# First batch of an attention-and-GLU kernel: q times kᵀv with 128 tokens a matmul, other warm matmuls, and a changed order of the first steps

## The chip, the cores and the metric

The kernel runs on one core of one Trainium2 chip, in fp32 throughout. The core has TensorE (matmuls, with a separate instruction that loads the stationary operand, the weights), VectorE, ScalarE, GpSimd and SyncE, which each take their instructions in order from a queue of their own, and 16 DMA engines. In the profile they are PE (matmul) and PEld (weight load), DVE, ACT, POOL and SP; a q behind a name is the engine's queue, where it issues a DMA or waits. The metric is the device time of one execution in microseconds (us). Of the kernel before, three executions gave 999.26, 999.58 and 1000.35 us, median 999.58.

## The reference

```
kv  = einsum('bhsd,bhse->bhde', k, v)            # 8 batches, 8 heads, 576 tokens, 64 wide
out = einsum('bhsd,bhde->bhse', q, kv)
rms = sqrt(mean(out * out, axis=-1) + 1e-6)
x   = out / rms * g_norm                         # to 4608 tokens by 512
y   = (sigmoid(x @ w_gate) * (x @ w_val)) @ w_out   # 512 -> 1536 -> 512
```

q, k and v come as float32. The three weights come as float64 and are passed as 64-bit words; the kernel makes float32 of them itself.

## The kernel before

The tokens are worked in chunks of 512 (`G`), nine of them. For all but the first chunk the two layers use a scheme with fewer products (`first_layer_fast`, L983, and `second_layer_fast`, L1085); the first chunk goes through plain matmuls of 128 by 512 (class `Plain`, L621, and `second`, L859), because the weights are still being converted then. The change touches only what comes before that: the attention of the first batch and the first conversions.

**Attention of the first batch.** Its eight heads are four pairs, n = 0 to 3, and `attention(n, ...)` has eleven steps for a pair. `KV` (L302) sums kᵀv over six groups of 96 tokens, one head on each half of the array's columns, and `KVO` (L306, VectorE) copies the result into `kvq`. `Q` (L312) transposes q through TensorE, and `QO` (L317, ScalarE) copies it to `qT`, with channels on partitions and tokens along the row. `U` (L329) multiplies: its stationary operand is a slice of `qT`, its moving operand the 64 by 64 kᵀv of one head, so the result has tokens on partitions. `SQ` (ScalarE), `SUM` (VectorE), `ROOT` (ScalarE) and `NORM` (VectorE, L346 and L348) make the norm; `X` (L356) transposes the result through TensorE, and `XO` (L365, ScalarE) copies it into `xT`, from which the layers read: pair m gives the m-th 128 channels. In `U` each matmul takes 64 tokens (`PH`): ten slices of tokens (`2 * NU`, the last one overlapping) for two heads, 20 matmuls of 64 by 64, in turn on the four quarters of the array.

**Warm matmuls.** `warmN` (L677) stands for N matmuls whose result nobody reads, with the 128 by 128 identity as both operands. They keep TensorE busy between real steps.

**Conversion.** Unit u is a staged pair of weight blocks (gate and value block of the same 128 hidden features, 128 by 512 each). Its five VectorE steps c.0 to c.4 (L195, L213, L225, L229, L236) and two ScalarE steps a.0 and a.1 (L200, L218) make float32 of it. `gu.i` and `vu.i` are the gate half and the value half of step i alone. Three staging buffers are in use; `w1` to `w4` (`load_unit`) issue the loads of units 1 to 4 on SP's queue, and `w3` and `w4` reuse the buffers of units 0 and 1. Later units are converted from `convert_step`, at places written out by hand among the plain matmuls.

**Order.** The string `order` (L654) fixes the order in which all this is recorded, and with that the order within each engine's queue. `b0.i.m` is one plain matmul of the first hidden block (i = 0 gate, 1 value; m the 128 channels it sums over, so it needs `XO` of pair m). After the string, the loop at L848 runs the plain matmuls of the other hidden blocks; block 1 needs unit 1 converted.

Of the kernel before, what the change touches and what calls it, by code (L numbers as in the profile page):

```python
# [10 lines left out]
FP32 = mybir.dt.float32  # L11
# [9 lines left out]
def kernel(  # L21
# [155 lines left out]
    def convert(u):  # L177
        kind, f = units[u]
        vec = nc.vector
        d = {}  # L180

        def s0(some=slice(None)):

            if kind == "gv":
                g, r = divmod(f, NF2)
                m = w1[:, r // 2, 2 * NMT * (r % 2):2 * NMT * (r % 2 + 1), g]
                for i, name in enumerate(("wg", "wv")):
                    w[name, f] = m[:, NMT * i:NMT * i + NMT]
            else:
                t = w2[:, f:f + 2, :]  # L190
                for i in range(2):
                    w["wo", f + i] = t[:, i]
                m = by_block(t.rearrange("p i f -> p (i f)"))
            d["m"] = m
            vec.tensor_scalar(out=m.bitcast(U32)[:, some], in0=words(u)[1][:, some], scalar1=0x000FFFFF, scalar2=None,  # L195
                              op0=ALU.bitwise_and)

        def a0():
            m = d["m"]
            nc.scalar.activation(out=m, in_=m.bitcast(U32), func=AF.Identity, scale=2.0 ** -20, bias=one)  # L200

        def s1(some=slice(None)):


            if "p" in d:
                t = None
            elif u < 15:
                t = raw.tile([P, UW], U32, tag="cz", name="cz", bufs=2)
            else:
                t = at_ps()[:, 0:2].rearrange("p r c -> p (r c)").bitcast(U32)  # L210
            if t is not None:
                d["p"] = by_block(t)
            vec.tensor_scalar(out=d["p"][:, some], in0=words(u)[1][:, some], scalar1=20, scalar2=0x7FF, op0=ALU.logical_shift_right,  # L213
                              op1=ALU.bitwise_and)

        def a1():
            p = d["p"]
            nc.scalar.activation(out=p.bitcast(I32), in_=p, func=AF.Relu, scale=2.0 ** 23, bias=exp_off)  # L218

        def s2():  # L220

            m = d["m"]
            if u > 2:
                load_unit(u - 1 + NST, (1,))
            vec.scalar_tensor_tensor(out=m, in0=words(u)[0], scalar=2.0 ** -52, in1=m, op0=ALU.mult, op1=ALU.add)  # L225

        def s3():
            p = d["p"]
            vec.scalar_tensor_tensor(out=p, in0=words(u)[1], scalar=0x80000000, in1=p, op0=ALU.bitwise_and,  # L229
                                     op1=ALU.bitwise_or)  # L230

        def s4():

            m, p = d["m"], d["p"].bitcast(FP32)
            if kind == "gv":
                vec.scalar_tensor_tensor(out=m, in0=m, scalar=g_col, in1=p, op0=ALU.mult, op1=ALU.mult)  # L236
            else:
                vec.tensor_tensor(out=m, in0=m, in1=p, op=ALU.mult)
            if u > 1:
                load_unit(u + NST, (0,))  # L240

        return {"c": [s0, s1, s2, s3, s4], "a": [a0, a1]}
# [48 lines left out]
    def attention(n, at_ps):  # L291

        b, m = divmod(n, NHP)
        d = {}
        kv = kvq[:, m // 2, m % 2]

        def kv_mm():
            d["kv"] = ps = at_ps("kv")
            for j in range(NJ):
                js = slice(HD * j, HD * j + HD)  # L300
                for e in range(2):
                    nc.tensor.matmul(ps[HD * e:HD * e + HD, 0, 0:HD], pairs[n]["k"][:, e, js], pairs[n]["v"][:, e, js],  # L302
                                     start=(j == 0), stop=(j == NJ - 1))

        def kv_out():
            nc.vector.tensor_copy(out=kv, in_=d["kv"][:, 0, 0:HD])  # L306

        def q_mm():
            d["q"] = ps = at_ps("q")
            for j in range(NJ):  # L310
                c0 = NP * (j % JH)
                nc.tensor.transpose(ps[:, j // JH, c0:c0 + NP], pairs[n]["q"][:, j].rearrange("p e d -> p (e d)"),  # L312
                                    ident[0:NP, 0:NP])

        def q_out():
            d["qT"] = qTs[:, S * (n % 2):S * (n % 2) + S]
            nc.scalar.copy(out=d["qT"].rearrange("p (i n) -> p i n", i=2), in_=d["q"][:, :, 0:JH * NP])  # L317

        def u_mm():


            ps = at_ps("u")
            d["u"] = ps[:, :, 0:NU * HD]
            for i in range(2 * NU):
                t0 = min(PH * i, S - PH)
                r = PH * (i % 2)
                for e in range(2):
                    es = slice(HD * e, HD * e + HD)
                    nc.tensor.matmul(d["u"][r:r + PH, e, HD * (i // 2):HD * (i // 2) + HD],  # L329
                                     d["qT"][es, t0:t0 + PH], kv[es], start=True, stop=True)  # L330

        def u_square():
            d["sq"] = sqs[:, NU * P * (n % 2):NU * P * (n % 2 + 1)].rearrange("p (e c) -> p e c", e=2)
            nc.scalar.activation(out=d["sq"], in_=d["u"], func=AF.Square)

        def u_sum():
            d["ms"] = sb.tile([P, 2, NU], FP32, tag="ms", name="ms")
            nc.vector.tensor_reduce(out=d["ms"].rearrange("p e i -> p (e i)"),
                                    in_=d["sq"].rearrange("p e (i d) -> p (e i) d", d=HD), axis=AX.X, op=ALU.add)

        def u_root():
            nc.scalar.activation(out=d["ms"], in_=d["ms"], func=AF.Sqrt, bias=eps, scale=1.0 / HD)

        def u_norm():

            nc.vector.reciprocal(d["ms"], d["ms"])  # L346
            d["xn"] = d["sq"].rearrange("p e c -> p (e c)")
            nc.vector.tensor_tensor(out=d["xn"].rearrange("p (i e d) -> p e i d", e=2, d=HD),  # L348
                                    in0=d["u"].rearrange("p e (i d) -> p e i d", d=HD),
                                    in1=d["ms"].unsqueeze(3).to_broadcast([P, 2, NU, HD]), op=ALU.mult)  # L350

        def x_mm():
            d["x"] = ps = at_ps("x")
            for i in range(NU):
                bank, c0 = divmod(P * i, UX)
                nc.tensor.transpose(ps[:, bank, c0:c0 + P], d["xn"][:, P * i:P * i + P], ident)  # L356

        def x_out():

            s0 = 0  # L360
            while s0 < S:
                c, o = divmod(S * b + s0, G)
                i, r = divmod(s0, UX)
                n_ = min(G - o, (UX if i == 0 else S - UX) - r)
                nc.scalar.copy(out=chunk(c)[:, m, o:o + n_], in_=d["x"][:, i, r:r + n_])  # L365
                s0 += n_

        return [kv_mm, kv_out, q_mm, q_out, u_mm, u_square, u_sum, u_root, u_norm, x_mm, x_out]
# [264 lines left out]
    def plain(c, u, ps, steps_at):  # L633
# [18 lines left out]


    order = """  # L654
        w1 w2 warm8 KV0 warm2 Q0 KVO0 QO0 warm4 U0 SQ0 KV1 Q1 SUM0 ROOT0 KVO1 QO1 NORM0 g0.0 g0.1 warm3 U1 SQ1 X0 XO0
        SUM1 ROOT1 v0.0 a0.0 NORM1 v0.1 a0.1 warm12 KV2 Q2 c0.2 KVO2 QO2 X1 XO1 c0.3 U2 SQ2 c0.4 w3 KV3 Q3 KVO3 QO3
        SUM2 ROOT2 g1.0 g1.1
        NORM2 b0.0.0 U3 SQ3 b0.1.0 X2 XO2 v1.0 SUM3 ROOT3 a1.0 v1.1 a1.1 NORM3 b0.0.1 b0.1.1 b0.0.2 X3 XO3 b0.1.2
        c1.2 c1.3 c1.4 w4 b0.0.3 b0.1.3
    """  # L660
    blk = None
    for token in order.split():
# [3 lines left out]
        if name == "b":  # L666
            blk = blk or Plain(0, F_ORDER[0], (warm, pair_kv))
            blk.mm(n[1], n[2])
        elif name in ("c", "a"):
            conversion[f][name][n[1]]()  # L670
        elif name in ("g", "v"):
            conversion[f]["c"][n[1]](slice(NMT * (name == "v"), NMT * (name == "v") + NMT))
        elif name == "w":
            load_unit(f)
        elif name == "warm":
            for _ in range(f):
                nc.tensor.matmul(warm[:, 0:P], ident, ident, start=True, stop=True)  # L677
        else:
            a[f][steps[name]]()
            if token == f"Q{NE - 1}":  # L680
                first_ctx.__exit__(None, None, None)
                hp = ctx.enter_context(tc.tile_pool(name="hp", bufs=1))
                h_main = [hp.tile([P, 4 * NT, P], FP32, name=f"h{j}") for j in range(N3)]
                h_more = hp.tile([P, N3, 3 * NT, P], FP32, name="h_more")
# [529 lines left out]
```

## Time and profile before

| | |
|---|---|
| median of three executions | 999.58 us |
| profiled execution | 998.65 us |
| its span, first to last instruction | 996.9 us |
| matmuls busy | 989.6 us, 99% |
| weight loads busy | 816.1 us, 82% |
| VectorE / ScalarE / GpSimd busy | 718.5 / 343.0 / 615.2 us |

The span starts with the first instruction on any engine; what lies around it belongs to the execution's time too. A matmul in fp32 leaves two records of PE and two of PEld, a transpose through TensorE one of each. A record's length holds its passage through the array, so neighbouring records overlap, and how far apart they start tells more than how long each is.

The early transfers on SP's queue, with the time at which they had landed (us from the span's start):

| load | landed |
|---|---|
| k, v of pair 0 | 3.75, 4.86 |
| q of pair 0, head by head | 5.46, 7.14 |
| weights of unit 0, gate and value | 11.53, 13.46 |
| k, v of pair 2 | 14.67, 15.65 |
| k, v of pair 3 | 17.70, 18.84 |
| weights of unit 1, gate and value | 22.02, 23.52 |

### The profile page before, as it was taken

How to read it: one execution, taken by the hardware profiler on the slowest of the kernel's cores; microseconds unless marked ns; L12 is line 12 of the kernel's file. 1: busy time of each engine (PE TensorE's matmuls, PEld its weight loads, DVE VectorE, ACT ScalarE, POOL GpSimd, SP SyncE). 2: the span in 40 equal slices, each digit the busy share in tenths (PEclk: the TensorE clock that was granted, in tenths of full speed). 3: DMA queues.
4: the chain of work that ended last, by engine and by line, in shares of the span. 5: the costliest groups of instructions: out<-in, count | busy, mean ns of one | idle time of the engine just before them, and what ended most of it. 6: DMA issues, size and time to landing. Idle time of an engine off the chain costs nothing.

```text
span 996.9 us, 16586 instructions
## 1 busy us (share of the span) xinstructions
PE 989.6 (99%) x5958; PEld 816.1 (82%) x5958; DVE 718.5 (72%) x1189; ACT 343.0 (34%) x621; POOL 615.2 (62%) x991
## 2 busy tenths in 40 slices
PE   8999999999999999999999999999999999999998
PEld 7454447888888888888888888888888888888887
DVE  5989999898768766784777576866686566756672
ACT  4576323661145213530344124411442133213320
POOL 1239997798259635865286708771686359734963
PEclk9999999999999999999999999999999999999999
DMA  9995415763889568646975677656954455545614
GB/s 279 278 285 179 151 42 154 231 218 96 300 265 293 158 187 279 193 157 200 276 225 162 201 211 259 180 168 196 288 171 147 147 191 195 159 148 170 214 48 123
DMA packets 149522, 194.96 MB, mean 196 GB/s; under 512 B 79840, under 2 KB 121696, under 8 KB 149440
## 3 DMA queue, kind: packets, MB, share of 16 engines
q0 software_dynamic: 22512, 116.41, 35.2%
q1 hardware_dynamic: 120848, 75.66, 27.2%
q10 hardware_dynamic: 6080, 1.84, 0.8%
q8 instruction: 47, 0.77, 0.3%
q14 instruction: 35, 0.29, 0.1%
HBM read 160.04 MB, written 25.56 MB: 186 GB/s over the span
## 4 chain that ended last, share of the span: by engine, by line
PE 92%; DVE 4%; SPq 1%; ACT 1%; issue 1%; DMA 1%; DVEq 0%
PE mm L983 54%; PE mm L1085 27%; PE mm L621 5%; PE mm L859 3%; PE at L453 2%; DVE cz L229 1%; DVE w L225 1%; PE at L403 1%; DMA st<-in_moe_w_gate_dram 1%; PE mm L403 1%; SPq L100 1%; DVE w L195 1%; SPq L93 1%; DVE cz L213 0%; ACT sqs L497 0%
## 5 line engine op out<-in xcount | busy, mean ns | idle before, releaser
L983 PE MATMUL mm<-xs,w 128*128 128x256 f32 x1428 | 331.3, 380 | 0.0
L983 PEld LDWEIGHTS mm<-xs,w 128*128 128x128 f32 x1428 | 271.5, 190 | 36.4
L983 PE MATMUL mm<-xT,w 128*128 128x256 f32 x948 | 230.6, 380 | 0.0
L983 PEld LDWEIGHTS mm<-xT,w 128*128 128x128 f32 x948 | 180.0, 190 | 24.7 <-issue 0.5
L805 POOL DMA_DIRECT2D w<-kept x84 | 46.8, 557 | 203.9 <-PE mm L983 200.3
L953 DVE TENSOR_TENSOR sg<-sg,mm 128x512 f32<-128x512 f32 (+1 forms) x176 | 100.7, 599 | 88.4 <-PE mm L983 35.0
L1085 PE MATMUL mm<-w,h 128*128 128x256 f32 x630 | 142.8, 379 | 0.0
L1085 PEld LDWEIGHTS mm<-w,h 128*128 128x128 f32 x630 | 119.9, 190 | 16.0
L949 ACT COPY temps<-mm 128x512 f32<-128x512 f32 (+1 forms) x128 | 66.0, 537 | 187.2 <-PE mm L1085 94.7
L945 POOL TENSOR_TENSOR h<-h,sg 128x512 f32<-128x512 f32 x72 | 96.7, 1360 | 44.0 <-ACT sg L942 28.0
L758 POOL TENSOR_TENSOR h<-h 128x128 f32<-128x128 f32 x216 | 110.9, 526 | 16.6 <-DVE h_more L758 13.1
L1085 PE MATMUL mm<-w,h_more 128*128 128x256 f32 x474 | 108.2, 379 | 0.0
L942 ACT ACTIVATE sg<-sg 128x512 f32<-128x512 f32 x96 | 59.7, 630 | 126.9 <-DVE sg L953 126.9
L1085 PEld LDWEIGHTS mm<-w,h_more 128*128 128x128 f32 x474 | 90.2, 190 | 12.1
L949 ACT COPY sg<-mm 128x512 f32<-128x512 f32 (+1 forms) x112 | 57.1, 510 | 87.7 <-PE mm L1085 45.3
L758 POOL TENSOR_TENSOR h_more<-h 128x128 f32<-128x128 f32 x120 | 58.4, 490 | 34.9 <-DVE h L945 30.5
L953 DVE TENSOR_TENSOR temps<-temps,mm 128x512 f32<-128x512 f32 (+1 forms) x96 | 59.4, 619 | 26.0 <-PE mm L1085 16.8
L621 PE MATMUL mm<-xT,w 128*128 128x512 f32 x176 | 77.2, 596 | 0.1
L953 DVE TENSOR_TENSOR temps<-mm,temps 128x512 f32<-128x512 f32 (+1 forms) x64 | 39.8, 622 | 51.9 <-PE mm L1085 23.9
L949 ACT COPY h<-mm 128x512 f32<-128x512 f32 x48 | 28.1, 585 | 129.9 <-PE mm L983 129.9
L953 DVE TENSOR_TENSOR sg<-mm,sg 128x512 f32<-128x512 f32 (+1 forms) x64 | 39.7, 620 | 42.2 <-PE mm L1085 22.2
L621 PEld LDWEIGHTS mm<-xT,w 128*128 128x128 f32 x176 | 32.9, 190 | 40.0 <-issue 37.0
(154 smaller groups left out, 1292.1 us busy)
## 6 DMA issues: line engine op xcount, KB each, us to landing
w<-kept POOLq DMA_DIRECT2D x42, 896.0 KB, 5.5
w<-kept POOLq DMA_DIRECT2D x90, 384.0 KB, 4.6
w<-kept POOLq DMA_DIRECT2D x42, 768.0 KB, 5.2
out_dram<-sg SPq DMA_DIRECT2D x119, 64.0 KB, 1.7
q<-in_q_dram SPq DMA_DIRECT2D x96, 72.0 KB, 5.1
xT<-xTs SPq DMA_DIRECT2D x96, 72.0 KB, 4.7
st<-in_moe_w_gate_dram SPq DMA_DIRECT2D x12, 512.0 KB, 6.7
st<-in_moe_w_val_dram SPq DMA_DIRECT2D x12, 512.0 KB, 7.3
```

Of the source, the lines that this page charges most:

```text
L403: nc.tensor.matmul(ps[m][HD * g:HD * g + HD, e], mains[2 * m + g, "k"][:, c], mains[2 * m + g, "v"][:, c], start=(b == 2 and e == 0 and j ...
L453: nc.tensor.matmul(to[HD * e:HD * e + HD], qTs[HD * g:HD * g + HD, c:c + HD], kvq[HD * g:HD * g + HD, m, e], start=True, stop=True)
L621: nc.tensor.matmul(self.ps[i], w[("wg", "wv")[i], self.f][:, m, :], xT[self.c][:, m, :], start=(m == 0), stop=(m == NMT - 1), skip_group_c ...
L758: ops.append((eng, lambda v=v, x=x, sign=sign, y=y, eng=eng: eng.tensor_tensor(out=h_form(v, j), in0=h_form(x, j), in1=h_form(y, j), op=op ...
L805: nc.gpsimd.dma_start(out=granule(g)[:, 0:n], in_=kept1[g // NPA % N3, g % NPA][:, 0:n])
L859: nc.tensor.matmul(ps[t], gv[0, f][:, P * t:P * t + P], w["wo", f], start=(f == 0), stop=(f == NFT - 1), skip_group_check=True)
L942: nc.scalar.activation(out=o["o" + step[1]], in_=o["o" + step[1]], func=AF.Sigmoid)
L945: mult.tensor_tensor(out=o[x], in0=o[x], in1=o[y], op=ALU.mult)
L949: nc.scalar.copy(out=o[out_], in_=o[expr])
L953: tt(out=o[out_], in0=o[x], in1=o[y], op=ALU.add if sign == "+" else ALU.subtract)
L983: nc.tensor.matmul(regions[name][1][:, g], ws[:, g], xf[c][wv], start=(new and g == 0), stop=True, skip_group_check=True)
L1085: nc.tensor.matmul(regions[name][1], h_form(hv, j), ws[:, j], start=(used[i] and j == 0), stop=(j == N3 - 1), skip_group_check=True)
```

## The change

Four things change; what is computed stays the same.

1. `U` takes 128 tokens a matmul where 128 are left: four slices of 128 and, for the last 64 tokens, two matmuls of 64 on the two halves of the partitions, as before. For two heads that is 12 matmuls for 20.
2. A warm matmul has 64 moving columns for 128, with the same 128 by 128 identity as stationary operand. The numbers change from 8, 2, 4, 3, 12 to 16, 4, 9, 6, 26.
3. `NORM2` is recorded ahead of `g1.0` and `g1.1`, and `b0.1.2` ahead of `X3` and `XO3`.
4. The last conversion step of unit 1, `c1.4`, becomes two steps of half the width, `g1.4` and `v1.4`. `s4` gets an argument for that.

```diff
-        def s4():
+        def s4(some=slice(None)):
-            m, p = d["m"], d["p"].bitcast(FP32)
+            m, p = d["m"][:, some], d["p"].bitcast(FP32)[:, some]
...
             d["u"] = ps[:, :, 0:NU * HD]
-            for i in range(2 * NU):
-                t0 = min(PH * i, S - PH)
-                r = PH * (i % 2)
-                for e in range(2):
-                    es = slice(HD * e, HD * e + HD)
-                    nc.tensor.matmul(d["u"][r:r + PH, e, HD * (i // 2):HD * (i // 2) + HD],
-                                     d["qT"][es, t0:t0 + PH], kv[es], start=True, stop=True)
+            for i in range(NU):
+                for r, n_ in ((0, P),) if i < NK4 else ((0, PH), (PH, PH)):
+                    t0 = min(P * i, S - PH)
+                    for e in range(2):
+                        es = slice(HD * e, HD * e + HD)
+                        nc.tensor.matmul(d["u"][r:r + n_, e, HD * i:HD * i + HD], d["qT"][es, t0:t0 + n_], kv[es],
+                                         start=True, stop=True)
...
     order = """
-        w1 w2 warm8 KV0 warm2 Q0 KVO0 QO0 warm4 U0 SQ0 KV1 Q1 SUM0 ROOT0 KVO1 QO1 NORM0 g0.0 g0.1 warm3 U1 SQ1 X0 XO0
-        SUM1 ROOT1 v0.0 a0.0 NORM1 v0.1 a0.1 warm12 KV2 Q2 c0.2 KVO2 QO2 X1 XO1 c0.3 U2 SQ2 c0.4 w3 KV3 Q3 KVO3 QO3
-        SUM2 ROOT2 g1.0 g1.1
-        NORM2 b0.0.0 U3 SQ3 b0.1.0 X2 XO2 v1.0 SUM3 ROOT3 a1.0 v1.1 a1.1 NORM3 b0.0.1 b0.1.1 b0.0.2 X3 XO3 b0.1.2
-        c1.2 c1.3 c1.4 w4 b0.0.3 b0.1.3
+        w1 w2 warm16 KV0 warm4 Q0 KVO0 QO0 warm9 U0 SQ0 KV1 Q1 SUM0 ROOT0 KVO1 QO1 NORM0 g0.0 g0.1 warm6 U1 SQ1 X0 XO0
+        SUM1 ROOT1 v0.0 a0.0 NORM1 v0.1 a0.1 warm26 KV2 Q2 c0.2 KVO2 QO2 X1 XO1 c0.3 U2 SQ2 c0.4 w3 KV3 Q3 KVO3 QO3
+        SUM2 ROOT2 NORM2 g1.0 g1.1 b0.0.0 U3 SQ3 b0.1.0 X2 XO2 v1.0 SUM3 ROOT3 a1.0 v1.1 a1.1 NORM3 b0.0.1 b0.1.1
+        b0.0.2 b0.1.2 X3 XO3 c1.2 c1.3 g1.4 v1.4 w4 b0.0.3 b0.1.3
     """
...
-                nc.tensor.matmul(warm[:, 0:P], ident, ident, start=True, stop=True)
+                nc.tensor.matmul(warm[:, 0:PH], ident, ident[:, 0:PH], start=True, stop=True)
```

## The prediction

> **What bounds the kernel now.** I read three things in turn: the sums by stretch of time, the chain of waits, and TensorE's instructions in order of time.
>
> The sums by stretch (stretch, its length, busy time of TensorE's matmuls with their number, of its weight loads, of the other engines):
>
> ```profile
> 16.30:30.80 14.50, 13.73 (x173) 8.20 (x172) 12.90 (x20) 10.39 (x20) 7.70 (x11) 1.00 1.10 295
> 30.80:128.20 97.40, 97.20 (x512) 46.05 (x512) 90.42 (x96) 51.53 (x89) 64.63 (x57) 1.00 0.72 213
> ```
>
> From 30.80 to 128.20 us TensorE is without matmuls for 0.20 us of 97.40. After that the chain of waits (start, us, what) is TensorE's own work to the end:
>
> ```profile
> 27.98 2.73 PE mm L621 x6
> 30.71 0.08 issue
> 30.80 1.53 PE mm L621 x3
> ...
> 128.22 27.73 PE mm L859 x64
> ```
>
> Between 80 and 128 us the chain runs through VectorE, but TensorE waits only once there, 0.31 us at 128.22 for the last w conversion of L238. So from 30.80 us on there is next to nothing in which a delay could be made up: what moves the start of the stream at 30.80 moves the end as much, less 0.3 us at most. The change lies wholly ahead of that point. There, in order of time (start, us, instruction, wait before it):
>
> ```profile
> 1.36 3.78 PE L677 MATMUL mm<-ident 128*128 128x128 f32 x16 [1.36 <-POOL ident masks.py:199]
> 5.07 0.97 PE L302 MATMUL mm<-v,k 96*64 96x64 f32 x24
> 5.97 0.71 PE L677 MATMUL mm<-ident 128*128 128x128 f32 x4
> 7.28 0.69 PE L312 MATMUL two<-ident,q 96*128 96x96 f32 x6 [0.60 <-DMA q<-in_q_dram]
> 7.80 1.08 PE L677 MATMUL mm<-ident 128*128 128x128 f32 x8
> 8.82 0.81 PE L329 MATMUL two<-kvq,qTs 64*64 64x64 f32 x40
> ...
> 12.17 0.81 PE L329 MATMUL two<-kvq,qTs 64*64 64x64 f32 x40 [0.35 <-ACT qTs L317]
> 12.91 0.76 PE L356 MATMUL two<-ident,sqs 128*128 128x128 f32 x5
> 13.51 2.84 PE L677 MATMUL mm<-ident 128*128 128x128 f32 x24
> 16.29 0.92 PE L302 MATMUL mm<-v,k 96*64 96x64 f32 x24
> ...
> 24.12 0.74 PE L356 MATMUL two<-ident,sqs 128*128 128x128 f32 x5 [0.44 <-DVE sqs L348]
> 24.69 2.74 PE L621 MATMUL mm<-xT,w 128*128 128x512 f32 x6
> 27.27 0.71 PE L356 MATMUL two<-ident,sqs 128*128 128x128 f32 x5
> ```
>
> The reader is to see that TensorE is nearly closed here too, and that the warm matmuls (L677) stand in its queue ahead of real work. The 24 records ahead of 16.29 end just where the next k^T v (L302) starts; its v had landed at 15.65.
>
> **The price of a warm record.** A fp32 matmul leaves two records here, each with its own weight load. `ident` is both operands: 128 weight columns and, so far, 128 moving columns. The change halves the moving columns and about doubles the number: 8, 2, 4, 3, 12 (29 matmuls, 58 records) become 16, 4, 9, 6, 26 (61, 122 records). The weights stay 128 columns. What one costs, the trace does not show. From below it is bounded by the k^T v rows with 64 moving and 64 weight columns: records on one part of the array come 0.058 us apart ((0.97-0.27)/12 for pairs on two halves). From above by the old warm record, (2.84-0.28)/23 = 0.112 us. Which of the two it is nearest to, the weight loads tell (min/median/max ns):
>
> ```profile
> L677 PEld LDWEIGHTS mm<-ident x58: 186/192/334, 1.4 to 16.0; 128*128 128x128 f32 x58
> ...
> L302 PEld LDWEIGHTS mm<-v,k x96: 132/138/183, 5.1 to 20.0; 96*64 96x64 f32 x96
> ...
> L329 PEld LDWEIGHTS two<-kvq,qTs x160: 129/135/136, 8.8 to 22.4; 64*64 64x64 f32 x160
> ```
>
> 64 more columns cost 192-138 = 54 ns, whatever the number of rows, so a load of 128 columns occupies the path about 0.108 us. The same shows where loads run with nothing ahead of them:
>
> ```profile
> 28.71 0.30 PEld L621 LDWEIGHTS mm<-xT,w 128*128 128x128 f32 x2 [0.70 <-ACT xT L365]
> ```
>
> Two loads of 0.19 us each take 0.30 together: the second starts 0.11 after the first. In the old warm record load and matmul are equally long and lie beside each other. With half the moving columns the matmul shrinks, the load does not, and the loads follow one another at 0.11. I take 0.112 us; 0.058 stays as the other end. (The transposes of L356 load 128 columns in a median of 141 ns, but they leave one record per matmul, not two, so they are another form.)
>
> At the start everything is slower: 16 records take from 1.36 to 5.07, about 0.22 us each, loads up to 334 ns. The records are at full speed from 5.2 on.
>
> **The same for q times k^T v** (L329). Before: 40 records on four quarters of the array, ten rounds of 0.058, 0.74 us to the next instruction. After: 8 matmuls with 128 weight columns (qT is the weight side) on two row halves, so 8 rounds of two records, and two rounds of four as before. At 0.112 for a wide round: 0.90+0.12 = 1.02 against 0.58, +0.44; at 0.058 it is nothing. I take +0.4 for each of the four.
>
> **The sum, along TensorE's queue:**
> - warm16: until 5.2 us 18 of 32 records pass at 0.213, then 14 at 0.112: k^T v of pair 0 starts at 6.9 for 5.07, +1.85.
> - warm4: 4 records more, +0.45; but the 0.60 us wait for q (landed 7.14) is swallowed, and 0.15 around it. The transposes start at 8.85: +1.55.
> - warm9: 10 more, +1.1: first q(k^T v) at 11.5, +2.65; itself +0.4: +3.05.
> - warm6: 6 more, +0.65, less the 0.35 wait for qTs, which vanishes: +3.35; second q(k^T v) +0.4: +3.75.
> - warm26: 28 more, 28 x 0.112 = +3.1: k^T v of pair 2 at 23.1 for 16.29, +6.85.
> - third and fourth q(k^T v), +0.8: the second b0 matmul ends at 31.1 for 23.5, +7.6.
> - NORM2 ahead of g1.0, g1.1: those two had waited for the transfer landing at 22.02, and NORM2 (0.20+0.82) stood behind them, so X2 waited 0.6 us for it (0.44 by the row above, the rest issue). With TensorE this late NORM2 is long done: -0.6, +7.0.
> - b0.1.2 moved ahead of X3: in the old order this matmul (0.86) covered the copies XO3; now TensorE stands about 0.7 us between X3 and b0.0.3: +0.7, +7.7. VectorE's and ScalarE's work for pair 3 (ready some 2 us earlier than X3 starts) gives no wait.
> - the last step of unit 1 in halves: 1.28 us becomes two of 0.64 to 0.72 (128x512 against 128x1024 is 0.42 against 0.69 at L195), and the first half suffices for the gate matmuls. Before, the stream waited 0.26 us for the whole step; after, the half is done near 37, ahead of TensorE: -0.2. The 0.1 us more on VectorE hides under the same lateness; without that cover it is 0.1.
>
> So the stream starts at 38.3 for 30.80, +7.5. Conversion of unit 2 on VectorE starts some 7.1 us late (its order follows the late pairs), so it does not hold the stream; the one wait at 128.22 can give back up to 0.3. The loads on SP that wait for VectorE (unit 3 after s3 of unit 0) start about 7 us later and are needed as much later; SP's and POOL's first loads wait on earlier transfers, not on TensorE, and have landed by then.
>
> One thing is to add: when full speed comes. It came 3.8 us after the first matmul, and what followed had slack (the q wait). After the change nothing follows with slack, and TensorE's moving side is only half filled. Each microsecond later costs half a microsecond: from nothing to 1.9 us (once more as long at half speed); I add 0.7. In all +8.2: span 996.9+8.2 = 1005.1. The profiled execution took 998.65, 1.75 around its span, so 1006.9; the median of the runs shown is 0.9 above it: **1007.8**.
>
> The Trainium skill ("TensorE: Matmul & The Clock Gate", Part 1) says the array runs at half clock until a free-running window of about 3.4 us was busy. This trace's first slow records, 1.36 to 5.2, fit that; by it the switch may come up to 3 us later from run to run, 1.5 us of time, inside what I add and the range.
>
> **Rivals.**
> *Records priced by their moving columns (not slower).* If a load overlaps more than one matmul, so that a record costs 0.058, the place is the same five warm groups: 64 against 128 columns at double the number cost 122 x 0.058 = 7.1 against 6.5, most of it in warm26 and warm9 (+0.5), q(k^T v) nothing; X2 then starts at 23.9 for 24.12, the uncovered copy costs 0.7, the halved step returns 0.2: +0.2, 1000. It decides below about 0.065 us a record. For it: the matmul side alone; against it: loads of 128 columns 0.11 apart.
> The Trainium skill (same page, "Back-to-back issue gap") has a table by moving columns alone in which 64 cost less than half of 128; by it this rival would come true, though the section itself says that both instructions set the spacing in a stream.
> *Clock stays at half through the first stage.* If half-filled matmuls do not count as busy, the 23 us of TensorE's work between 5.2 and 28 double: about +22 more, 1030. Against it: from 5.2 to 28 the records stay fast across idle gaps of 0.5 us.
> *The delay is made up later.* Transfers run ahead meanwhile, but the stretch to 128.20 has 0.2 to 0.3 us of waits: no more than that, 1007.5; counted with the forecast.
>
> **How the numbers follow.** Forecast 0.87, rival by moving columns 0.09, half clock 0.04. About 0.2% (2 us) can be told from no change here. Slower is forecast and half clock, 0.91; of the remainder 0.07 is no change, and 0.02 faster, for what a cheaper record and the earlier X2 might give. Forecast's own range is 1005 (records at 0.107, q(k^T v) as before, no late clock) to 1010 (clock later by the full 3.8 us, wide rounds dearer); for 8 in 10 I take 1004 to 1012.
>
> **What would show it.** Right: the 52 warm records of the fifth group 5.8 us long, their loads 0.11 apart; pair 2's k^T v near 23; q(k^T v) about 1.2 us; TensorE idle 0.7 between X3 and b0.0.3; the stream from 38; from there on all rows as before, shifted. Wrong: 52 records in 3 us, or pair 2 at 16 to 17; a stretch to the last w conversion shorter than 97.4 would mean that time was made up.

## The result, and the profile after

The changed kernel takes 1026.65 us, median of six executions (1025.90 to 1029.73). The kernel before, beside it, takes 999.51, median of six. The ratio is 1.0278, with a 95% interval of 1.0264 to 1.0293: 27 us slower. The forecast was 1007.8 with a range of 1004 to 1012, so it had the sign and a third of the size; the rival to which it gave a chance of 0.04, TensorE at half clock through the first stage, had given 1030.

The profiled execution has a span of 1027.0 us, 30.1 more than before (996.9). That is 3 us more than the medians differ by, because the profiled execution of before lies 0.9 us below its median and the changed kernel's 2.1 above. TensorE's instructions in order of time, changed kernel (start, us, instruction, wait before it):

```profile
1.36 7.09 PE L676 MATMUL mm<-ident 128*128 128x64 f32 x32 [1.36 <-POOL ident masks.py:199]
8.38 1.55 PE L302 MATMUL mm<-v,k 96*64 96x64 f32 x24
...
16.51 2.39 PE L329 MATMUL two<-kvq,qTs 64*128 64x64 f32 x24
18.83 1.55 PE L302 MATMUL mm<-v,k 96*64 96x64 f32 x24
20.31 1.22 PE L312 MATMUL two<-ident,q 96*128 96x96 f32 x6
...
27.41 11.19 PE L676 MATMUL mm<-ident 128*128 128x64 f32 x52
38.53 1.55 PE L302 MATMUL mm<-v,k 96*64 96x64 f32 x24
...
42.23 2.39 PE L329 MATMUL two<-kvq,qTs 64*128 64x64 f32 x24
44.56 1.55 PE L302 MATMUL mm<-v,k 96*64 96x64 f32 x24
46.03 1.22 PE L312 MATMUL two<-ident,q 96*128 96x96 f32 x6
47.05 1.97 PE L621 MATMUL mm<-xT,w 128*128 128x512 f32 x2
48.95 2.39 PE L329 MATMUL two<-kvq,qTs 64*128 64x64 f32 x24
51.27 2.07 PE L621 MATMUL mm<-xT,w 128*128 128x512 f32 x2
53.14 1.27 PE L356 MATMUL two<-ident,sqs 128*128 128x128 f32 x5
54.20 3.65 PE L621 MATMUL mm<-xT,w 128*128 128x512 f32 x8
57.69 0.71 PE L356 MATMUL two<-ident,sqs 128*128 128x128 f32 x5
59.13 3.27 PE L621 MATMUL mm<-xT,w 128*128 128x512 f32 x7 [0.74 <-ACT xT L365]
```

The rows that the change does not touch are the thermometer. The 24 kᵀv records (L302) took 0.92 us before from the second pair on; here all four pairs take 1.55. The five transposes (L356) take 1.27 to 1.33 up to 53.14, and 0.71 at 57.69, as before. So TensorE ran at half speed up to about 54 us instead of 5. The loads of the warm matmuls say the same (min/median/max ns; their median was 192 before):

```profile
L676 PEld LDWEIGHTS mm<-ident x122: 288/333/337, 1.4 to 38.1; 128*128 128x128 f32 x122
```

The trace's own record of the clock starts with the rise to full speed, at 5.2 us before and at 54.3 after. What the page prints as the granted clock is of no use here: having nothing before the rise, it prints full speed. The sums by stretch, changed kernel (length, PE, PEld, DVE, ACT, POOL, granted clock, DMA share, GB/s):

```profile
16.51:38.53 22.02, 22.02 (x148) 21.20 (x147) 6.32 (x12) 5.49 (x10) 0.00 (x0) 1.00 0.45 125
59.13:158.50 99.37, 99.23 (x517) 46.78 (x518) 92.28 (x98) 53.38 (x92) 61.74 (x52) 1.00 0.65 206
```

In the first line clock and busy times look perfect, with matmuls busy for all of 22.02 us and loads for 21.20, and yet the clock is at half and, under the warm matmuls and the wide q(kᵀv), only half of the time goes to moving columns. The second line shows the other half of the reasoning at work: from the stream on TensorE has no idle time (0.14 us), and the delay of 30.4 us at the start of b0.0.3 (59.13 for 28.71) is, to 0.3 us, the 30.1 at the end.

One execution in the experiments (e3 below, 1022.65 us) is left out of the comparison there; its trace was not taken.

### The profile page after: what moved, and what is told of

The parts are those of the page before. It is cut to its first block, busy times and chain, and to the rows that moved or that the text cites. A ratio compares the mean times of both kernels' runs of the same rounds, so it can differ in the third digit from the quotient of the medians.

```text
span 1027.0 us, 16587 instructions
## 1 busy us (share of the span) xinstructions
PE 1020.8 (99%) x5958; PEld 844.2 (82%) x5958; DVE 718.9 (70%) x1190; ACT 343.0 (33%) x621; POOL 615.6 (60%) x991
## 4 chain that ended last, share of the span: by engine, by line
PE 95%; DVE 3%; ACT 1%; issue 1%; POOL 0%; DVEq 0%; POOLq 0%
PE mm L982 53%; PE mm L1084 26%; PE mm L621 5%; PE mm L858 3%; PE mm L676 3%; PE at L453 2%; PE two L329 1%; DVE cz L229 1%; DVE w L225 1%; PE at L403 1%; PE mm L403 1%; PE mm L302 1%; DVE w L195 1%; PE two L312 0%; PE two L356 0%
## 5 line engine op out<-in xcount | busy, mean ns | idle before, releaser
L952 DVE TENSOR_TENSOR temps<-temps,mm 128x512 f32<-128x512 f32 (+1 forms) x96 | 59.4, 618 | 27.1 <-PE mm L1084 16.8
```

The lines of the kernel that those rows point to most:

```text
L952: tt(out=o[out_], in0=o[x], in1=o[y], op=ALU.add if sign == "+" else ALU.subtract)
```

## The experiments

All times are medians; "before" is the kernel before in the same job. The rises are from the trace's record of the clock.

| | what runs | us | before | ratio, 95% interval | full speed from, us |
|---|---|---|---|---|---|
| – | changed kernel | 1026.65 | 999.51 | 1.0278, 1.0264 to 1.0293 | 54.3 |
| e1 | changed, old warm matmuls | 1000.41 | 999.55 | 1.0009, 1.0000 to 1.0018 | 7.3 |
| e2 | before, new warm matmuls | 1013.23 | 999.55 | 1.0155, 1.0127 to 1.0184 | 20.2 |
| e3 | changed, first group old | 1004.79 | 999.55 | 1.0052, 1.0037 to 1.0068 | 4.8 |
| e4 | before, new q(kᵀv) | 1000.05 | 999.55 | 1.0006, 0.9997 to 1.0015 | 6.9 |
| e5 | before, first group new | 1005.26 | 999.20 | 1.0071, 1.0056 to 1.0086 | 15.0 |
| e9 | changed, fifth group old | 1015.21 | 999.56 | 1.0155, 1.0140 to 1.0171 | 31.2 |
| e14 | changed, 80 moving columns | 1027.65 | 999.56 | 1.0282, 1.0265 to 1.0299 | 48.5 |
| e10 | changed, 96 moving columns | 1007.57 | 999.20 | 1.0090, 1.0075 to 1.0105 | 6.5 |
| e12 | changed, 128 moving columns, new numbers | 1007.16 | 999.20 | 1.0085, 1.0070 to 1.0100 | 6.4 |
| e11 | changed, 64 weight columns | 1000.97 | 999.20 | 1.0020, 1.0010 to 1.0029 | 6.1 |

**e1, e2, e4: which part of the change does it.** e1 is the changed kernel with the old warm matmuls:

```diff
-        w1 w2 warm16 KV0 warm4 Q0 KVO0 QO0 warm9 U0 ... warm6 U1 ... warm26 KV2
+        w1 w2 warm8 KV0 warm2 Q0 KVO0 QO0 warm4 U0 ... warm3 U1 ... warm12 KV2
...
-                nc.tensor.matmul(warm[:, 0:PH], ident, ident[:, 0:PH], start=True, stop=True)
+                nc.tensor.matmul(warm[:, 0:P], ident, ident, start=True, stop=True)
```

> The changed kernel with the old warm matmuls (128 moving columns; 8, 2, 4, 3, 12 of them); the new q(k^T v), order and halved step stay. Theory G, the clock: the warm matmuls with 64 moving columns keep TensorE at half clock until the stream of 512-column matmuls; with the old ones full speed comes at 5.2 us, and what is left is four q(k^T v) at +0.4, the uncovered copy +0.7, less 0.8 for NORM2 and the halved step: about 1001. Rival U, the wide q(k^T v) keeps the clock down too: full speed comes later than 20 us, over 1008.

e2 makes the opposite edit in the kernel before, and e4 puts the new loop of `u_mm` there and nothing else.

> The kernel before with the new warm matmuls alone (64 moving columns; 16, 4, 9, 6, 26). Theory G: the clock stays at half until the first plain matmuls, 1020 to 1023 (the changed kernel's 1026.7 less four q(k^T v), which take about 1.2 us in the old form at half clock and 2.3 in the new one). Rival U: with the old q(k^T v) the clock rises near 9 us as before, 1006 to 1008. Rival P, what I had predicted: no clock, only 0.112 us a record: 1006.

> The kernel before with the new q(k^T v) alone. If a round with 128 weight columns costs 0.112 us: 0.4 us for each of the four, less 0.35 that waited for qTs anyway, 1000.5 to 1001.2. If a round costs what its moving columns cost: no change. Clock up at 5.2 us in both.

e1 comes out at 1000.41: without the new warm matmuls 26 of the 27 us are gone. But e2 costs only 14 of them, and e4 about 0.5, which is no clear difference. The parts do not add up, and the rows of e2's traced execution, the fastest of its four (1009.87 to 1019.25), show why (start, us, instruction):

```profile
16.51 1.35 PE L329 MATMUL two<-kvq,qTs 64*64 64x64 f32 x40
17.79 1.55 PE L302 MATMUL mm<-v,k 96*64 96x64 f32 x24
19.27 1.13 PE L312 MATMUL two<-ident,q 96*128 96x96 f32 x6
20.24 1.48 PE L677 MATMUL mm<-ident 128*128 128x64 f32 x12
...
22.99 5.92 PE L677 MATMUL mm<-ident 128*128 128x64 f32 x52
```

At 20.2 us, behind 3.7 us of q(kᵀv), kᵀv and transposes without a warm matmul between, the clock comes up, and the 52 warm records take 5.92 us, not 11.19. In the changed kernel the same stretch opens with the wide q(kᵀv), whose matmul side is by the same reckoning half filled (64 moving against 128 weight columns, 2.39 us), and only 2.5 filled us remain: no rise. So neither of my theories was right alone: in these two traces the warm matmuls keep the clock down, and the wide q(kᵀv), nearly free by itself, takes away the next occasion for it to rise.

**e3, e5, e9: when it rises and whether it stays.** One group of the changed kernel goes back to its old form (e3 the first, `warm16` to 8 of 128 columns; e9 the fifth, `warm26` to 12), or one group of the kernel before takes the new form (e5, the first):

```diff
-        w1 w2 warm16 KV0
+        w1 w2 full8 KV0
...
+        elif name == "full":
+            for _ in range(f):
+                nc.tensor.matmul(warm[:, 0:P], ident, ident, start=True, stop=True)
```

> The changed kernel with its first warm group alone in the old form (8 matmuls of 128 columns for 16 of 64). Theory G with a clock that stays up once it is up: full speed at 5.2 us, the rest at 0.112 us a record: about 1005 to 1006. Theory G with a clock that falls again in half-filled groups (the fifth is 5.8 us long): 1012 to 1022, and the records of the fifth group 0.21 us apart.

> The kernel before with its first warm group alone in the new form (16 matmuls of 64 moving columns for 8 of 128). Theory G: full speed does not come at 5.2 us; TensorE is filled from k^T v of pair 0 (near 8.4 us) on, so it comes 3.5 to 7 us after that, at 12 to 16 us. The first group is then 3.3 us longer, and 4 to 7 us more pass at half speed: 1004 to 1008. If the first group must be filled once and for all, the clock stays down to the plain matmuls: over 1015.

> The changed kernel with its fifth warm group alone in the old form (12 matmuls of 128 columns for 26 of 64). Theory G: half speed up to that group, which starts at 27.4 us and at half speed lasts 5.1 us; full speed comes within it or just behind it, at 31 to 36 us, and holds. The start is as late as in the changed kernel up to 27.4, then the group is about 7 us shorter and 15 us of half-speed work behind it take about 8: 1009 to 1014. If the clock must come up in the first group or not at all before the stream: 1019 to 1022.

e3's fifth group and the kᵀv behind it:

```profile
15.49 5.92 PE L679 MATMUL mm<-ident 128*128 128x64 f32 x52
21.34 0.92 PE L302 MATMUL mm<-v,k 96*64 96x64 f32 x24
```

Once up, the clock stays up in this execution through 5.9 us of half-filled records: they do not bring it up, but they do not lose it either. Another execution of e3 took 1022.65 us, near the changed kernel; without a trace it stays open whether the clock came late there or fell again. In e5 and e9 it rises 6.6 us after the first filled work and 3.8 us after it, and 1005.26 is as expected for e5. e9, expected at 1009 to 1014, took 1015.21; its kᵀv of pair 2 starts at 31.98 for 38.53, and the rest of the gain is work at full speed behind it.

The length of a filled stretch does not decide alone. In the changed kernel 3.7 us (38.53 to 42.23) and 4.4 us (44.56 to 48.95) of filled work pass at half speed, and the rise at 54.3 comes after 3.0. The trace's record of the clock shows what else counts: every stretch that ends inside a trace lasts a whole number of 3.413 us. Full speed lasts 989.87 us before (290 of them), 972.80 in the changed kernel (285) and 986.45 in e2 (289). So the clock changes only at the ends of windows of 3.41 us, and where these lie differs from execution to execution: before and e8, with the same work on TensorE up to 5 us, rise at 5.2 and at 7.4. Counted back from their rises, the changed kernel and e2 share a window from 16.8 to 20.2, and they have the same work up to 16.51; with the narrow q(kᵀv) this window brings the rise, with the wide one it does not. The two longer stretches of the changed kernel lie across ends of windows (40.65, 44.06 and 47.47). The spread of e2 and the 1022.65 of e3 may come from the position of the windows too, but no trace shows it.

How full a window must be is not settled for work other than the warm matmuls. In e5 the window from 8.15 to 11.56 holds, but for its first 0.23 us, kᵀv, full warm matmuls and transposes, and brings no rise; the last one of the changed kernel (50.89 to 54.30) begins with 0.38 us of the wide q(kᵀv) and does.

e5's trace also has a fall: TensorE stands still for 2.10 us from 716.2, with no wait on record, the window to 718.12 has 1.52 us of matmuls in 3.42, and the next 3.41 us run at half speed. That execution took 1007.76, 2.5 us above e5's median.

**e10, e14, e12, e11: what counts as filled.** Only the operands of the warm matmul change; numbers and everything else are the changed kernel's:

```diff
-                nc.tensor.matmul(warm[:, 0:PH], ident, ident[:, 0:PH], start=True, stop=True)
+                nc.tensor.matmul(warm[:, 0:96], ident, ident[:, 0:96], start=True, stop=True)         # e10; e14 80, e12 128
+                nc.tensor.matmul(warm[0:PH, 0:PH], ident[:, 0:PH], ident[:, 0:PH], start=True, stop=True)   # e11
```

> The changed kernel with 96 moving columns in each warm matmul for 64, same numbers of them. A record stays as long as its weight load (0.21 us at half speed, 0.11 at full), and its moving side is filled for 75% of it instead of 50%. If the share that decides lies between 50 and 75%: full speed at 5 to 9 us and 1006 to 1009. If it lies above 75%: as the changed kernel, 1025 to 1029.

> The changed kernel with 80 moving columns in each warm matmul: filled for 62% of a record, between the 50% that leaves the clock down and the 75% that brings it up (1007.6). Up at 5 to 9 us and 1006 to 1009 if the deciding share lies below 62%; 1025 to 1029 if above; between the two, or spread from run to run, if it lies close by.

> The changed kernel with 128 moving columns in each warm matmul and the new, doubled numbers of them: the moving side is filled, a record as long as with 64 columns. Theory G: full speed at 5 to 7 us, 52 records of the fifth group in 5.8 to 5.9 us, and the sum that I had predicted, 1005 to 1008. If the number of instructions or records keeps the clock down: 1025 or more.

> The changed kernel with 64 weight columns in each warm matmul for 128, 64 moving columns and the numbers as they are. Load and matmul are equally long again, so the moving side is filled, over half the columns of the array. If the filled time counts: a record every 0.107 us at first and 0.058 later, full speed at 5 to 9 us, and about 1001, as with the old warm matmuls. If the share of the array in use counts: the clock stays down; records stay at 0.107, and the time lies between 1008 and 1020.

First group and the kᵀv behind it, in e14, then in e10:

```profile
1.37 7.12 PE L676 MATMUL mm<-ident 128*128 128x80 f32 x32 [1.37 <-POOL ident masks.py:199]
8.41 1.55 PE L302 MATMUL mm<-v,k 96*64 96x64 f32 x24
```

```profile
1.36 6.25 PE L676 MATMUL mm<-ident 128*128 128x96 f32 x32 [1.36 <-POOL ident masks.py:199]
7.54 0.92 PE L302 MATMUL mm<-v,k 96*64 96x64 f32 x24
```

With 80 columns the matmul fills 62% of the record that its load sets, and the clock stays down until 48.5: 1027.65, as with 64. With 96, 75%, it rises at 6.5 us: 1007.57, and 128 columns are worth hardly more (1007.16). For the warm matmuls the step lies between 62 and 75%. e11 tells what fills: there the weights have 64 columns, so load and matmul are equally long again over half the array's columns, and the clock rises at 6.1. It is the time in which columns move that counts, not the share of the array's columns in use, the number of instructions or the loads, which are busy nearly all the time in every one of these. Whether the rows in use count was not tried.

e12 is also the test of my sum. It has the doubled records, the new q(kᵀv), order and halved step, and an ordinary clock: 1007.16, against 1007.8 forecast; beside its own before it is 8.0 us slower (interval 7.0 to 10.0), where the sum had 8.2. Its rows at full speed are close to those of the sum (start, us, instruction, wait before it):

```profile
18.10 5.97 PE L676 MATMUL mm<-ident 128*128 128x128 f32 x52
24.00 0.92 PE L302 MATMUL mm<-v,k 96*64 96x64 f32 x24
...
36.30 0.71 PE L356 MATMUL two<-ident,sqs 128*128 128x128 f32 x5
37.75 7.56 PE L621 MATMUL mm<-xT,w 128*128 128x512 f32 x17 [0.74 <-ACT xT L365]
```

So the 27.1 us divide into 19.2 for the half clock (27.14 less the 7.96 of e12), 7.1 for the 64 additional records (e12 less e1, each beside its own before; 64 x 0.112 = 7.2) and 0.9 for the rest (e1).

**e8 and e13: do two of the parts make a faster kernel?** e8 is the kernel before with two edits of the change, e13 has 9 warm matmuls for 12 in the fifth group besides:

```diff
-        SUM2 ROOT2 g1.0 g1.1
-        NORM2 b0.0.0 U3
+        SUM2 ROOT2 NORM2 g1.0 g1.1
+        b0.0.0 U3
...
-        c1.2 c1.3 c1.4 w4
+        c1.2 c1.3 g1.4 v1.4 w4
```

> The kernel before with NORM2 ahead of g1.0 and g1.1, and the last step of unit 1 in halves; nothing else of the change. My sum: X2 no longer waits 0.6 us, and the stream no longer 0.26 for the whole step: 0.6 to 0.8 us faster, 998.4 to 998.9 beside a kernel before at 999.2 to 999.6. Rival: another wait takes their place (VectorE reaches the last step as late as before), no change.

> As the one before, with the fifth warm group at 9 matmuls for 12 (128 columns), 0.67 us less. The v that the next k^T v waits for had landed at 15.65, the group ended at 16.29: 0.3 to 0.6 us less again if TensorE sets the start of the stream; no further change if the third pair's q (landed near 16.9) or the conversion of unit 0 (20.2) does.

e8 took 998.82 beside 999.56 (ratio 0.9993, 0.9985 to 1.0002), e13 998.59 (0.9991, 0.9983 to 1.0000). The size is that expected of e8, but neither can be told from no change. Why it is not more, the rows of the traced execution of e13 show in part (start, us, instruction, wait before it):

```profile
21.87 0.81 PE L329 MATMUL two<-kvq,qTs 64*64 64x64 f32 x40
23.83 1.02 PE L621 MATMUL mm<-xT,w 128*128 128x512 f32 x2 [1.15 <-issue]
24.69 0.71 PE L356 MATMUL two<-ident,sqs 128*128 128x128 f32 x5
```

X2 no longer waits for NORM2, which ended at 23.09. In its place TensorE stands still 1.15 us ahead of b0.1.0, whose operands are long there, and the profile names no cause ("issue"). In e8 a stop of 0.88 us falls between two records of the fourth q(kᵀv), where no operand can be missing either. What TensorE waits for there was not tried and stays open. The shorter fifth group of e13 is paid back by two waits that before does not have there: 0.49 us for v at 15.89 and 0.32 for q at 17.12.

## Why the prediction was wrong

**The step that failed is the clock.** The text had: "One thing is to add: when full speed comes", and bounded it "from nothing to 1.9 us (once more as long at half speed)". It did so although the sentence before it said that the moving side would be only half filled. The clock did not come a little later: with the moving side of the warm matmuls filled for half of the time it stayed down up to 54.3 us, and it rose only there, among transposes and plain matmuls. That term, set at 0.7, measures 19.2 us plus the little that e12 has of it (full speed at 6.4 for 5.2 us).

**The reason given against the right rival was about something else.** "From 5.2 to 28 the records stay fast across idle gaps of 0.5 us" shows that the clock, once up, stays up across such gaps. e3's trace shows the same with half-filled records. It says nothing on what brings it up. The trace of before could not tell: all of its work ahead of 5.2 us is filled. With no row for or against, 0.04 was too little, and the range had to reach that rival.

**The Trainium skill's rule was read as a window only.** "TensorE: Matmul & The Clock Gate", Part 1, says that the default state is throttled and that activity over a free-running window of about 3.4 us releases it. The whole numbers of 3.413 us in this case's records of the clock agree with that window, and so do times from the start of filled work to the rise of 3.4 us (e3) and 6.6 us (e5); the 3.0 us of the changed kernel do so only if a window need not be filled to the last. I used the window for the delay, and not the condition that it must be busy.

**The sum along the queue was right in the main.** The price of a record, 0.112 us by its load, is confirmed where the clock is up: 52 records in 5.92 us in e3 ((5.92-0.28)/51 = 0.111), and the rival by moving columns (0.058) falls with it. Pair 2's kᵀv was to start at 23.1, before the term for the clock, and does at 24.00 in e12: the later rise (1.2 us at half speed, about 0.6) and the two dearer q(kᵀv) ahead of it (0.2 each) make up about the 0.9. The stream could be moved and the end followed, as the second stretch above shows.

**Smaller terms.** The wide q(kᵀv) was put at +0.4; in e4 from the start of the first to the next instruction it is 10.10-8.78 = 1.32 for 0.74, +0.58. The uncovered copy XO3 was put at 0.7 and is 0.74, named by the wait on L365 in the changed kernel, e1 and e12. NORM2's gain of 0.6 is there in e1, where X2 starts 0.96 us after b0.1.0 for 1.56 before; in e8 and e13 another stop takes its place. The halved step was put at -0.2, and in e1 the wait of 0.26 is gone. All of these together make 0.9 us in e1 (interval 0.0 to 1.8), where my sum, with four times 0.4, had 1.5.

## What to carry to other kernels

Warm matmuls have to keep columns moving: a weight load that is longer than its matmul fills the time and both busy rows, but with 64 or 80 moving columns to 128 weight columns it did not bring up the clock here, so make the moving side at least as wide as the weights. Judge the clock by a form that you know at both speeds (here 24 records in 0.92 or 1.55 us), not by a printed share that begins with the first rise. And before the clock is up, price each change by whether it still lets the clock come up, not by its own duration: an edit that is free alone can take the next occasion for it.

## What the runs showed of the hardware that was not expected

- Warm matmuls that move columns for 50 or 62% of the time leave TensorE at half clock for as long as they go on (11.2 us in one group); 75% bring it up (6.5 us, e10). Loads do not count (busy for 21.20 of 22.02 us), nor does the share of the array's columns (6.1 us, e11).
- The same 50% keep the clock up once it is up, for 5.9 us in e3's trace.
- The clock changes at the ends of windows of 3.413 us (full speed for 290, 285 and 289 of them before, in the changed kernel and in e2), whose position differs between executions (rise at 5.2 before, at 7.4 in e8, with the same work up to 5 us).
- A load of 128 fp32 columns costs 0.11 us a record however few columns move: 64, 96 and 128 moving columns give 52 records in 5.92 (e3), 5.94 (e10) and 5.97 us (e12).
- TensorE can stand still between matmuls with no wait on record: 0.88 us in e8, 1.15 in e13, 2.10 in e5, and the last cost a window of full speed.
